# Mixing two token tiles side by side with the sines, and loading the first q and k in four halves

## The chip, the cores and the metric

The kernel runs on one core of one Trainium2 chip. The metric is the device time of one execution in microseconds (us); smaller is better. Seven runs of the kernel before gave a median of 173.86 us, from 173.14 to 174.23.

## The reference

Banded attention (a window of 96 tokens and 8 global tokens) with a linear distance bias, followed by a layer that mixes tokens through cosines and sines. Softmax is written here in one line:

```python
def _attn_ref(q, k, v, n_global, n_local):      # q, k, v: [4, 8, 768, 64] f32
    scores = scale * np.matmul(q, k.transpose(0, 1, 3, 2))
    rel = pos[:, None] - pos[None, :]
    is_global = pos[None, :] < int(n_global)                 # 8
    is_local = (rel >= 0) & (rel < int(n_local))             # 96
    keep = is_global | is_local
    dist = np.where(is_global & ~is_local, float(n_local), np.abs(rel))
    scores = scores - slopes[:, None, None] * dist
    a = softmax of scores where keep
    return np.matmul(a, v)

x = attention output, heads side by side                     # [4, 768, 512]
theta = x @ w_theta
zr, zi = x * np.cos(theta), x * np.sin(theta)
y = einsum('ts,bsd->btd', w_tok_r, zr) + einsum('ts,bsd->btd', w_tok_i, zi)
u = x + y
return u + np.maximum(u @ w_ch, 0.0)
```

## The kernel before

There are four batches, eight heads in four pairs, and six token tiles of 128. Matrix work is in bf16. The kernel is a software pipeline: batch 0's attention runs first alone; then each batch's token mixing is interleaved with the next batch's attention.

*The opening (lines 97 to 145 and 519 to 550).* Two hardware queues load q and k of batch 0's heads 0 and 1 in f32: k on SyncE's queue (SP), q on ScalarE's (ACT), line 99. Everything else comes through GpSimd's queue (POOL), cast to bf16 on the way: the other heads' q and k, v in two halves (line 88), then the weights (lines 154 to 161), then q, k and v of batches 1 and 2 (lines 73 and 88). VectorE (DVE) builds distance tables. `cast0` makes bf16 of the first pair, one head on DVE and one on ACT; `turn0` transposes on TensorE (PE); `out0` copies the transposed pair out of PSUM; `kglob` makes copies of k with the global tokens in front (kG). `score_bias` puts the bias into PSUM by a matmul, `score_mms` adds the scores, `score_exp` takes the exp on ACT. A pair of heads has three chunks of scores.

*Attention of batch 0 (lines 551 to 585)* is a hand-written order. `vglob` makes vG, the copy of v with global tokens; it waits for v. `values` multiplies by v, divides by the sum (rec, L364) and writes x_sb (L366). `xtrans` transposes x_sb.

*Handover (lines 586 to 599).* `trans_w(0)` transposes the token weights of tile 0 (12 transposes on PE into two PSUM tiles, one copy each into w_tokT, L168). `theta(b, c, j)` makes theta for the token tile pair c (L398); for j = 1 or 3 it goes on with the sines on ACT (cs, L404) and the products with x on DVE (zri, L408). The hand-written order ends here; in the rest of the kernel a scheduler puts the instructions of each engine in order by the priorities of the program's text. `weave` sets this text order for batch 0's mixing (`main`) and batch 1's attention (`side`): it interleaves the two lists by weights, and starts `side` after a share s0 of `main`.

*Mixing.* `mix(b, tt, g)` adds four matmuls (L419) of tile tt to one PSUM tile; after three of them DVE adds x (u, L424). `utrans` transposes u, `chan` multiplies by w_ch (L447), adds u and stores (o_sb, L452; the store is issued on SP, L454). For batch 0, `trans_w(tt + 1)` follows the second part of tile tt's mix; for tiles 1 and 2 both copies are on DVE, for tiles 3 to 5 one is on ACT.

*Attention of batches 1 to 3.* `prep` turns q and k of a pair: copies on DVE (qkn, L231), transposes on PE, copies out on DVE (qT, L250) and ACT (kT, L252), then kG (L220, L222). After the exp, DVE multiplies by a table of the bias (e, L315 and L318). For these batches x_sb is transposed by a DMA issued on SP (L370). `theta(1, 0, 0)` needs the first three of the four transposed head pairs, `theta(1, 0, 1)` the fourth.

*PSUM* holds eight banks: the pool `big` has two buffers of two banks (scores, values of batches 1 to 3, theta of tile pairs 0 and 1), the pool `small` four buffers of one bank (everything else). A buffer is reused when its last reader is done.

Of the kernel before, what the change touches and what calls it, by code (L numbers as in the profile page):

```python
# [16 lines left out]
def kernel(  # L17
# [77 lines left out]
        mybir.EngineType.Pool, mybir.EngineType.SP}))  # L95

    qk32 = moe.tile([T, 2, 2, NT, D], FP, name="qk32", tag="zri", bufs=1)
    for i_, eng in ((1, nc.sync), (0, nc.scalar)):
        eng.dma_start(out=qk32[:, i_].rearrange("p h t d -> p h (t d)"),
                      in_=(q, k)[i_][0, 0:2].rearrange("h (p t) d -> p h (t d)", p=T))  # L100
    near = const.tile([T, 2 * T], FP)
    nc.gpsimd.iota(near, pattern=[[1, 2 * T]], base=0, channel_multiplier=-1,
                   allow_small_or_imprecise_dtypes=True)
# [56 lines left out]
                w_nat[wi, tt], w_nat[wi, tt + 1] = w2[:, 0], w2[:, 1]  # L160
        nc.gpsimd.dma_start(out=w_ch_bf, in_=moe_w_ch.rearrange("(c p) n -> p c n", p=T))

    def trans_w(tt, copy=nc.vector.tensor_copy):
        for wi in range(2):
            ps = ps_small([T, NT, T], BF)
            for st in range(NT):
                nc.tensor.transpose(ps[:, st, :], w_nat[wi, tt][:, st * T:(st + 1) * T], ident)
            (copy if wi else nc.vector.tensor_copy)(out=w_tokT[wi][:, :, tt * T:(tt + 1) * T], in_=ps)  # L168


# [212 lines left out]
    def theta(b, c, j):  # L383
        last0 = [(j_, NC - 1) for j_ in range(2)]
        part = {0: [(0, dc) for dc in range(NC - 1)],
                1: [(1, dc) for dc in range(NC - 1)] + last0,
                2: [(j_, dc) for j_ in range(2) for dc in range(NC - 1)],
                3: last0}[j]
        if c == 0 and j in (0, 2):
            zri[b] = moe.tile([T, 2, NT, DM], BF, name="zri", tag="zri", bufs=1)  # L390
        xT, xb = xT_sb[b], x_sb[b]
        last = c == NT // 2 - 1
        if j in (0, 2):
            pss["th", c] = [ps_small([T, DM], FP) for _ in range(2)] if last else ps_big()
        pb = pss["th", c]
        st = lambda j_: slice((2 * c + j_) * T, (2 * c + j_ + 1) * T)
        for j_, dc in part:
            nc.tensor.matmul(pb[j_] if last else pb[:, j_, :], lhsT=xT[:, dc, st(j_)],  # L398
                             rhs=w_theta_bf[:, dc, :], start=(dc == 0), stop=(dc == NC - 1))
        if j in (1, 3):  # L400
            cs = moe.tile([T, 2, 2, DM], BF, name="cs")
            for i_, bias in ((0, {"bias": halfpi}), (1, {})):
                for o, p_ in [(cs[:, i_, j_], pb[j_]) for j_ in range(2)] if last else [(cs[:, i_], pb)]:
                    nc.scalar.activation(o, p_, AF.Sin, **bias)  # L404
            n = 2 if b else 1
            for i_ in range(2):
                for j_ in range(0, 2, n):
                    nc.vector.tensor_mul(  # L408
                        zri[b][:, i_, 2 * c + j_:2 * c + j_ + n, :].rearrange("p j (g d) -> p j g d", g=NP),
                        xb[:, :, 2 * c + j_:2 * c + j_ + n, :].rearrange("p g j d -> p j g d"),  # L410
                        cs[:, i_, j_:j_ + n].rearrange("p j (g d) -> p j g d", g=NP))

    def mix(b, tt, g):
        if g == 0:
            pss["mix"] = ps_small([T, DM], FP)
        ps = pss["mix"]
        for st in (2 * g, 2 * g + 1):
            for wi in range(2):
                anchor["pe"] = nc.tensor.matmul(  # L419
                    ps, lhsT=w_tokT[wi][:, st, tt * T:(tt + 1) * T], rhs=zri[b][:, wi, st, :],  # L420
                    start=(st == 0 and wi == 0), stop=(st == NT - 1 and wi == 1)).ins
        if g == NT // 2 - 1:
            u_sb[b, tt] = moe.tile([T, DM], BF, name="u", bufs=6)
            anchor["dve"] = nc.vector.tensor_add(  # L424
                u_sb[b, tt].rearrange("p (g d) -> p g d", g=NP), x_sb[b][:, :, tt, :],
                ps.rearrange("p (g d) -> p g d", g=NP)).ins
# [99 lines left out]
    distances()  # L526
    diagonals(0)
    score_bias(0, 0)
    score_bias(0, 1)
    cast0(1, dve, 0)  # L530
    bias_table(0)
    cast0(1, act, 1)
    turn0(0, 1)
    cast0(0, dve, 0)
    cast0(0, act, 1)
    turn0(0, 0)
    diagonals(1)
    out0(0, 1, act, 0)
    out0(0, 1, dve, 1)
    out0(0, 0, act, 1)  # L540
    out0(0, 0, dve, 0)
    kglob(0, 0, 0, 1, act)
    score_mms(0, 0, 0)
    kglob(0, 0, 1, NT - 2, act)
    score_exp(0, 0, 0)
    turn0(1, 1)
    turn0(1, 0)
    score_mms(0, 0, 1)
# [42 lines left out]
    theta(0, 1, 2)  # L591
    xtrans(0, p, dve, 4, 6)
    theta(0, 0, 3)
    theta(0, 1, 3)
    theta(0, 2, 2)
    theta(0, 2, 3)
    for h in range(1, H):
        bias_table(h)
    manual.close()
# [4 lines left out]
    for b in range(B):  # L604
        nxt = b + 1 if b + 1 < B else None
        lag = 3
        th = [lambda c=c, j=j: theta(b, c, j) for c in range(NT // 2) for j in range(2)]
        pre = [lambda p=p: prep(1, p) for p in range(NP)] if b == 0 else []
        ahead = [[lambda p=p: prep(2, p) for p in range(NP // 2)], [lambda p=p: prep_dma(3, p) for p in range(1)],
                 [], []][b]  # L610
        order = rest[:1] + th[:4] + rest[1:2] + th[4:] + rest[2:] if b else []
        if b == 2:
            order[:0] = [lambda p=p: prep_dma(3, p) for p in range(1, NP)]
        if b == 1:
            order.insert(0, lambda: load_behind(3, xT_sb[1][0:1, NC - 1, 0:1]))
        for f in order:
            f()
        main = []
        for tt in range(NT):
            for g in range(NT // 2):  # L620
                if (b, tt) != (B - 1, NT - 1):
                    main.append((2048, lambda tt=tt, g=g: mix(b, tt, g)))
                if b == 0 and g == 1 and tt + 1 < NT:
                    main.append((1536, lambda tt=tt: trans_w(tt + 1, nc.scalar.copy if tt > 1 else nc.vector.tensor_copy)))
                if tt >= lag and g == 0 and (b, tt) != (B - 1, NT - 1):
                    main.append((2048, lambda tt=tt: chan(b, tt - lag)))
                if b == 0 and tt and g == 1:
                    main.append((512, lambda tt=tt: utrans(b, tt - 1)))
            if b and (b, tt) != (B - 1, NT - 1):
                main.append((0, lambda tt=tt: utrans(b, tt)))  # L630
        side = [(1536, f) for f in pre]
        if b == 0:
            side[:0] = [(0, lambda: load_all_v(2))]
            side.append((0, lambda: (alloc_qk(3), load_qk_tokens(3, 0, H // 2))))
        side += attention_steps(nxt, ahead) if nxt else []
        weave(main, side, 0.3 if b == 0 else 0.0, 0.9)
        rest = [lambda tt=tt, b=b: chan(b, tt) for tt in range(NT - lag, NT)]
        if b == 0:
            rest.insert(1, lambda b=b: utrans(b, NT - 1))
# [44 lines left out]
```

The softmax here doesn't subtract the row's maximum and nothing guards it: scores larger than these inputs give would overflow.

## Time and profile before

| what | value |
|---|---|
| median of 7 runs | 173.86 us |
| the profiled execution, its own time | 173.69 us |
| its span in the profile | 171.6 us |
| PE busy | 159.8 us (93%), 1534 matmuls |
| DVE busy | 124.8 us (73%) |
| ACT busy | 101.3 us (59%) |
| POOL busy | 39.8 us (23%) |
| granted PE clock | full |
| moved by DMA | 25.93 MB, mean 151 GB/s |
| chain that ended last | PE 61%, DVE 16%, DMA 9%, ACT 7%, POOL 4% |
| costliest line | L419 (mix), 288 matmuls of 380 ns |

A line of a timeline gives the start, the duration (of the group, if several are merged), the engine, the line of the kernel, the operation, what is written from what, and in brackets the idle time before it and what ended it. A matmul's duration is that of its whole passage; matmuls overlap, so the spacing of their starts says what one costs. In a line of stretches the engines' busy times stand in the order PE, PE weight loads, DVE, ACT, POOL, then the granted clock, the DMA share and GB/s. Times on the timeline count from the start of the span.

### The profile page before, as it was taken

Reading aid. Unit: us, or ns where it says so; the run is one execution under the profiler, and the core shown is the slowest. Engines: PE = TensorE matmul, PEld = TensorE weight load, DVE = VectorE, ACT = ScalarE, POOL = GpSimd, SP = SyncE. Lnnn points to the kernel's source line nnn. Section 1 sums busy time; section 2 is a strip of 40 time slices with the busy share of each in tenths; the row PEclk is TensorE's granted clock in tenths of the full one; section 3 lists DMA queues with packets and bytes.
Section 4 is the critical chain, followed back from the end, with each engine's and each line's share of the span. In section 5 each row is a group of like instructions: output and inputs, shape, how many; then the busy total and the mean of one; then the engine's idle time right before and its main releaser. Section 6 shows DMA issues by size and latency. Waiting matters only on the chain.

```text
span 171.6 us, 3733 instructions
## 1 busy us (share of the span) xinstructions
PE 159.8 (93%) x1534; PEld 84.1 (49%) x1534; DVE 124.8 (73%) x265; ACT 101.3 (59%) x130; POOL 39.8 (23%) x45
## 2 busy tenths in 40 slices
PE   7489889989999999999999999989999999999991
PEld 2255456445755565445555464434454644444440
DVE  6737877587999999787998788297786856624442
ACT  4698683999797596199954550979347309500010
POOL 8965437005094010299000000000000000000000
PEclk9999999999999999999999999999999999999999
DMA  4999999999999999999996577888245563323335
GB/s 154 193 170 178 208 210 208 205 204 177 155 204 181 177 138 195 157 123 165 167 128 115 138 172 168 123 152 245 33 78 139 94 157 89 122 49 103 96 92 183
DMA packets 75088, 25.93 MB, mean 151 GB/s; under 512 B 63168, under 2 KB 72128, under 8 KB 75072
## 3 DMA queue, kind: packets, MB, share of 16 engines
q0 software_dynamic: 45680, 12.45, 77.6%
q1 hardware_dynamic: 28976, 12.72, 33.4%
q10 hardware_dynamic: 416, 0.52, 0.9%
q8 instruction: 12, 0.20, 0.5%
q14 instruction: 4, 0.03, 0.1%
HBM read 25.69 MB, written 6.29 MB: 186 GB/s over the span
## 4 chain that ended last, share of the span: by engine, by line
PE 61%; DVE 16%; DMA 9%; ACT 7%; POOL 4%; issue 2%; DVEq 0%; SPq 0%; POOLq 0%
PE ps L419 31%; PE ps L447 10%; DMA vn<-in_v_dram 6%; PE pb L398 6%; PE pb L296 5%; PE pb L355 4%; ACT cs L404 4%; POOL qk L73 3%; DMA kT<-qk 2%; DVE qT L250 2%; PE ps L398 2%; DVE zri L408 2%; DVE o_sb L452 2%; ACT e L306 2%; PE ps L246 1%
## 5 line engine op out<-in xcount | busy, mean ns | idle before, releaser
L419 PE MATMUL ps<-zri,w_tokT 128*128 128x512 bf16 x288 | 71.1, 380 | 1.6 <-DVE zri L408 0.8
L306 ACT ACTIVATE e<-pb 128x1024 bf16<-128x1024 f32 (+1 forms) x48 | 43.7, 960 | 17.7 <-PE pb L296 17.1
L419 PEld LDWEIGHTS <-w_tokT 128*128 128x128 bf16 x288 | 26.0, 98 | 30.2 <-issue 2.4
L424 DVE TENSOR_TENSOR u<-x_sb,ps 128x512 bf16<-128x512 bf16 x24 | 16.4, 684 | 13.1 <-PE ps L419 13.1
L447 PE MATMUL ps<-w_ch_bf,uT 128*128 128x512 bf16 (+1 forms) x100 | 24.7, 371 | 0.0
L408 DVE TENSOR_TENSOR zri<-x_sb,cs 128x1024 bf16<-128x1024 bf16 (+1 forms) x30 | 16.7, 581 | 5.6 <-ACT cs L404 5.3
L404 ACT ACTIVATE cs<-pb,halfpi 128x1024 bf16<-128x1024 f32 x8 | 8.9, 1115 | 19.2 <-PE pb L398 19.2
L452 DVE SCALAR_TENSOR_TENSOR o_sb<-ps,u 128x512 f32<-128x512 f32 (+1 forms) x25 | 16.4, 663 | 3.6 <-PE ps L447 3.6
L296 PE MATMUL pb<-qT,kT 64*128 64x128 bf16 x224 | 15.1, 219 | 1.6 <-DVE qT L211 1.3
L315 DVE TENSOR_TENSOR e<-e,etab 128x1024 bf16<-128x1024 bf16 (+1 forms) x24 | 14.8, 619 | 2.3 <-ACT e L306 2.3
L438 ACT COPY uT<-ps 128x512 bf16<-128x512 bf16 x7 | 4.1, 587 | 20.6 <-PE ps L437 20.6
L296 PEld LDWEIGHTS <-kT 64*128 64x128 bf16 x224 | 8.7, 94 | 14.7 <-issue 11.8
L398 PE MATMUL pb<-w_theta_bf,xT 128*128 128x512 bf16 x64 | 15.0, 379 | 0.0
L355 PEld LDWEIGHTS <-e 128*128 128x128 bf16 x352 | 13.0, 97 | 3.8 <-issue 1.6
L398 PEld LDWEIGHTS <-xT 128*128 128x128 bf16 x96 | 9.0, 98 | 10.8 <-DMA xT<-x_sb 0.9
L447 PEld LDWEIGHTS <-uT 128*128 128x128 bf16 x100 | 9.2, 98 | 10.0 <-ACT uT L438 0.8
L88 POOL DMA_DIRECT2D vn<-in_v_dram x5 | 9.6, 1924 | 12.2 <-DVE vn L68 10.3
L296 PE MATMUL pb<-qT,kG 64*128 64x128 bf16 x128 | 11.6, 217 | 0.9 <-DVE rec L364 0.5
L366 DVE TENSOR_TENSOR x_sb<-pb,rec 128x768 bf16<-128x768 f32 x12 | 11.4, 954 | 0.4
L82 POOL DMA_DIRECT2D qk<-in_k_dram x8 | 8.8, 1095 | 6.0 <-DMA vn<-in_v_dram 6.0
L355 PE MATMUL pb<-vn,e 128*128 128x65 bf16 x168 | 9.9, 193 | 0.2 <-ACT e L306 0.2
L318 DVE TENSOR_TENSOR e<-e,etab 128x1024 bf16<-128x1024 bf16 x12 | 8.2, 687 | 2.4 <-ACT e L306 2.4
(73 smaller groups left out, 203.6 us busy)
## 6 DMA issues: line engine op xcount, KB each, us to landing
out_dram<-o_sb SPq DMA_DIRECT2D x23, 256.0 KB, 2.4
vn<-in_v_dram POOLq DMA_DIRECT2D x3, 768.0 KB, 22.5
qk<-in_q_dram POOLq DMA_DIRECT2D x2, 768.0 KB, 20.7
qk<-in_k_dram POOLq DMA_DIRECT2D x2, 768.0 KB, 23.2
w_nat<-in_moe_w_tok_r_dram POOLq DMA_DIRECT2D x3, 384.0 KB, 15.1
w_nat<-in_moe_w_tok_i_dram POOLq DMA_DIRECT2D x3, 384.0 KB, 14.3
vn<-in_v_dram POOLq DMA_DIRECT2D x2, 384.0 KB, 9.9
qk<-in_q_dram POOLq DMA_DIRECT2D x8, 96.0 KB, 9.5
```

Source lines behind the costliest of these rows:

```text
L296: nc.tensor.matmul(pb[:, hh, o:o + T], lhsT=lhsT, rhs=qT[R, (own, nxt)[part]], start=bool(b), stop=bool(b) or (jt == NT - 1 or (j == 1 and ...
L306: ins = nc.scalar.activation(e_c, pb[:, :, 0:n], AF.Exp, scale=scale).ins
L315: nc.vector.tensor_mul(e_c, e_c, tab[:, :, s0:s0 + n // T].rearrange("p a s n -> p a (s n)"))
L355: nc.tensor.matmul(o, lhsT=l_, rhs=r_, start=(i_ == 0), stop=(i_ == len(mms) - 1))
L366: nc.vector.tensor_mul(xv, po4[:, :, :, 0:D], rec.to_broadcast([T, n, nt, D]))
L398: nc.tensor.matmul(pb[j_] if last else pb[:, j_, :], lhsT=xT[:, dc, st(j_)], rhs=w_theta_bf[:, dc, :], start=(dc == 0), stop=(dc == NC - 1))
L404: nc.scalar.activation(o, p_, AF.Sin, **bias)
L408: nc.vector.tensor_mul(zri[b][:, i_, 2 * c + j_:2 * c + j_ + n, :].rearrange("p j (g d) -> p j g d", g=NP), xb[:, :, 2 * c + j_:2 * c + j_ ...
L419: anchor["pe"] = nc.tensor.matmul(ps, lhsT=w_tokT[wi][:, st, tt * T:(tt + 1) * T], rhs=zri[b][:, wi, st, :], start=(st == 0 and wi == 0), ...
L424: anchor["dve"] = nc.vector.tensor_add(u_sb[b, tt].rearrange("p (g d) -> p g d", g=NP), x_sb[b][:, :, tt, :], ps.rearrange("p (g d) -> p g ...
L447: nc.tensor.matmul(ps_c, lhsT=uT[:, dc, :], rhs=w_ch_bf[:, dc, i_ * n:(i_ + 1) * n], start=(dc == 0), stop=(dc == NC - 1))
L452: nc.vector.scalar_tensor_tensor(o_sb[:, cols], in0=ps_c, scalar=0.0, in1=u[:, cols], op0=ALU.max, op1=ALU.add)
```

## The change

The first q and k are loaded as four halves, q of both heads first, one head on each of the two queues; q is cast and turned ahead of k, and each is copied out of PSUM whole. In the handover `trans_w` gets a wide form: its two PSUM tiles lie in one buffer of `big`, and both copies are on DVE. The sines and products become a function of their own, `sines`. Token tiles 0 and 1 of batch 0 are mixed in turns in the hand-written order, with the weight transposes of tiles 1, 2 and 3 and the sines between them. The interleaved part begins with tile 2; for tiles 4 and 5 both copies are on DVE; `side` starts after 0.1 of `main` in place of 0.3.

```diff
--- before.py
+++ after.py
@@ -95,9 +95,10 @@
         mybir.EngineType.Pool, mybir.EngineType.SP}))
 
     qk32 = moe.tile([T, 2, 2, NT, D], FP, name="qk32", tag="zri", bufs=1)
-    for i_, eng in ((1, nc.sync), (0, nc.scalar)):
-        eng.dma_start(out=qk32[:, i_].rearrange("p h t d -> p h (t d)"),
-                      in_=(q, k)[i_][0, 0:2].rearrange("h (p t) d -> p h (t d)", p=T))
+    for i_ in range(2):
+        for h, eng in enumerate((nc.sync, nc.scalar)):
+            eng.dma_start(out=qk32[:, i_, h].rearrange("p t d -> p (t d)"),
+                          in_=(q, k)[i_][0, h].rearrange("(p t) d -> p (t d)", p=T))
     near = const.tile([T, 2 * T], FP)
     nc.gpsimd.iota(near, pattern=[[1, 2 * T]], base=0, channel_multiplier=-1,
                    allow_small_or_imprecise_dtypes=True)
@@ -160,11 +161,16 @@
                 w_nat[wi, tt], w_nat[wi, tt + 1] = w2[:, 0], w2[:, 1]
         nc.gpsimd.dma_start(out=w_ch_bf, in_=moe_w_ch.rearrange("(c p) n -> p c n", p=T))
 
-    def trans_w(tt, copy=nc.vector.tensor_copy):
-        for wi in range(2):
-            ps = ps_small([T, NT, T], BF)
+    def trans_w(tt, copy=nc.vector.tensor_copy, wide=False):
+        pb = big.tile([T, 2, 2 * 512], BF, name="pbw", tag="pb") if wide else None
+        tiles = [pb[:, wi, 0:S].rearrange("p (t n) -> p t n", t=NT) if wide else ps_small([T, NT, T], BF)
+                 for wi in range(2)]
+        for wi, ps in enumerate(tiles):
             for st in range(NT):
                 nc.tensor.transpose(ps[:, st, :], w_nat[wi, tt][:, st * T:(st + 1) * T], ident)
+            if not wide:
+                (copy if wi else nc.vector.tensor_copy)(out=w_tokT[wi][:, :, tt * T:(tt + 1) * T], in_=ps)
+        for wi, ps in enumerate(tiles if wide else ()):
             (copy if wi else nc.vector.tensor_copy)(out=w_tokT[wi][:, :, tt * T:(tt + 1) * T], in_=ps)
 
 
@@ -397,25 +403,29 @@
         for j_, dc in part:
             nc.tensor.matmul(pb[j_] if last else pb[:, j_, :], lhsT=xT[:, dc, st(j_)],
                              rhs=w_theta_bf[:, dc, :], start=(dc == 0), stop=(dc == NC - 1))
-        if j in (1, 3):
-            cs = moe.tile([T, 2, 2, DM], BF, name="cs")
-            for i_, bias in ((0, {"bias": halfpi}), (1, {})):
-                for o, p_ in [(cs[:, i_, j_], pb[j_]) for j_ in range(2)] if last else [(cs[:, i_], pb)]:
-                    nc.scalar.activation(o, p_, AF.Sin, **bias)
-            n = 2 if b else 1
-            for i_ in range(2):
-                for j_ in range(0, 2, n):
-                    nc.vector.tensor_mul(
-                        zri[b][:, i_, 2 * c + j_:2 * c + j_ + n, :].rearrange("p j (g d) -> p j g d", g=NP),
-                        xb[:, :, 2 * c + j_:2 * c + j_ + n, :].rearrange("p g j d -> p j g d"),
-                        cs[:, i_, j_:j_ + n].rearrange("p j (g d) -> p j g d", g=NP))
+        if j == 1:
+            sines(b, c)
+
+    def sines(b, c):
+        pb, xb, last = pss["th", c], x_sb[b], c == NT // 2 - 1
+        cs = moe.tile([T, 2, 2, DM], BF, name="cs")
+        for i_, bias in ((0, {"bias": halfpi}), (1, {})):
+            for o, p_ in [(cs[:, i_, j_], pb[j_]) for j_ in range(2)] if last else [(cs[:, i_], pb)]:
+                nc.scalar.activation(o, p_, AF.Sin, **bias)
+        n = 2 if b else 1
+        for i_ in range(2):
+            for j_ in range(0, 2, n):
+                nc.vector.tensor_mul(
+                    zri[b][:, i_, 2 * c + j_:2 * c + j_ + n, :].rearrange("p j (g d) -> p j g d", g=NP),
+                    xb[:, :, 2 * c + j_:2 * c + j_ + n, :].rearrange("p g j d -> p j g d"),
+                    cs[:, i_, j_:j_ + n].rearrange("p j (g d) -> p j g d", g=NP))
 
     def mix(b, tt, g):
         if g == 0:
-            pss["mix"] = ps_small([T, DM], FP)
-        ps = pss["mix"]
-        for st in (2 * g, 2 * g + 1):
-            for wi in range(2):
+            pss["mix", tt] = ps_small([T, DM], FP)
+        ps = pss["mix", tt]
+        for wi in range(2):
+            for st in (2 * g, 2 * g + 1):
                 anchor["pe"] = nc.tensor.matmul(
                     ps, lhsT=w_tokT[wi][:, st, tt * T:(tt + 1) * T], rhs=zri[b][:, wi, st, :],
                     start=(st == 0 and wi == 0), stop=(st == NT - 1 and wi == 1)).ins
@@ -526,23 +536,22 @@
     distances()
     diagonals(0)
     score_bias(0, 0)
-    score_bias(0, 1)
-    cast0(1, dve, 0)
     bias_table(0)
-    cast0(1, act, 1)
-    turn0(0, 1)
     cast0(0, dve, 0)
     cast0(0, act, 1)
     turn0(0, 0)
-    diagonals(1)
-    out0(0, 1, act, 0)
-    out0(0, 1, dve, 1)
-    out0(0, 0, act, 1)
-    out0(0, 0, dve, 0)
+    score_bias(0, 1)
+    cast0(1, dve, 0)
+    out0(0, 0, dve)
+    cast0(1, act, 1)
+    turn0(0, 1)
+    warm(2)
+    out0(0, 1, act)
     kglob(0, 0, 0, 1, act)
     score_mms(0, 0, 0)
-    kglob(0, 0, 1, NT - 2, act)
+    kglob(0, 0, 1)
     score_exp(0, 0, 0)
+    diagonals(1)
     turn0(1, 1)
     turn0(1, 0)
     score_mms(0, 0, 1)
@@ -591,9 +600,19 @@
     theta(0, 1, 2)
     xtrans(0, p, dve, 4, 6)
     theta(0, 0, 3)
+    sines(0, 0)
     theta(0, 1, 3)
     theta(0, 2, 2)
     theta(0, 2, 3)
+    trans_w(1, dve, True)
+    sines(0, 1)
+    for g in range(NT // 2):
+        for tt in range(2):
+            mix(0, tt, g)
+        if g < 2:
+            trans_w(2 + g, dve, True)
+        if g == 0:
+            sines(0, 2)
     for h in range(1, H):
         bias_table(h)
     manual.close()
@@ -616,16 +635,18 @@
         for f in order:
             f()
         main = []
-        for tt in range(NT):
+        for tt in range(0 if b else 2, NT):
             for g in range(NT // 2):
                 if (b, tt) != (B - 1, NT - 1):
                     main.append((2048, lambda tt=tt, g=g: mix(b, tt, g)))
-                if b == 0 and g == 1 and tt + 1 < NT:
-                    main.append((1536, lambda tt=tt: trans_w(tt + 1, nc.scalar.copy if tt > 1 else nc.vector.tensor_copy)))
+                if b == 0 and g == 1 and 4 <= tt + 2 < NT:
+                    main.append((1536, lambda tt=tt: trans_w(tt + 2)))
                 if tt >= lag and g == 0 and (b, tt) != (B - 1, NT - 1):
                     main.append((2048, lambda tt=tt: chan(b, tt - lag)))
-                if b == 0 and tt and g == 1:
+                if b == 0 and g == 1:
                     main.append((512, lambda tt=tt: utrans(b, tt - 1)))
+                if (b, tt, g) == (0, 2, 0):
+                    main.append((512, lambda: utrans(0, 0)))
             if b and (b, tt) != (B - 1, NT - 1):
                 main.append((0, lambda tt=tt: utrans(b, tt)))
         side = [(1536, f) for f in pre]
@@ -633,7 +654,7 @@
             side[:0] = [(0, lambda: load_all_v(2))]
             side.append((0, lambda: (alloc_qk(3), load_qk_tokens(3, 0, H // 2))))
         side += attention_steps(nxt, ahead) if nxt else []
-        weave(main, side, 0.3 if b == 0 else 0.0, 0.9)
+        weave(main, side, 0.1 if b == 0 else 0.0, 0.9)
         rest = [lambda tt=tt, b=b: chan(b, tt) for tt in range(NT - lag, NT)]
         if b == 0:
             rest.insert(1, lambda b=b: utrans(b, NT - 1))
```

## The prediction

> **What bounds the kernel now.** I read the slices of the page first, to see which engines are full where; then the busy time by stretch; then the chain of waits and the timeline around the places that the diff touches; last the landing time of single loads.
>
> ```profile
> PE   7489889989999999999999999989999999999991
> DVE  6737877587999999787998788297786856624442
> DMA  4999999999999999999996577888245563323335
> ```
>
> A slice is 171.6/40 = 4.29 us. The DMA engines are full up to slice 22, some 94 us; VectorE (DVE) is nearly full in slices 10 to 15, some 43 to 69 us; TensorE (PE) looks full from slice 10 on, but its busy time hides gaps. The stretches show who really is full:
>
> ```profile
> 36.00:42.00 6.00, 5.90 (x43) 2.91 (x41) 4.36 (x11) 5.97 (x10) 2.21 (x1) 1.00 1.60 192
> 42.00:48.00 6.00, 5.87 (x81) 4.58 (x79) 6.00 (x17) 4.43 (x8) 1.23 (x2) 1.00 2.84 162
> 48.00:54.00 6.00, 5.96 (x80) 3.14 (x78) 6.00 (x14) 5.51 (x7) 5.01 (x5) 1.00 1.38 201
> 54.00:60.00 6.00, 5.87 (x81) 3.27 (x78) 5.96 (x14) 3.81 (x5) 0.82 (x1) 1.00 2.38 172
> 60.00:66.00 6.00, 5.48 (x92) 3.96 (x87) 5.93 (x13) 5.91 (x9) 0.83 (x1) 1.00 2.03 144
> 66.00:72.00 6.00, 6.00 (x47) 3.17 (x45) 4.99 (x11) 1.61 (x3) 0.21 (x2) 1.00 1.40 205
> ```
>
> After the length come PE, PE weight loads, DVE, ScalarE (ACT), GpSimd (POOL). DVE works 23.89 of the 24 us from 42 to 66. PE is not full there: a 512-column matmul in a packed row costs 0.216 us (40 in 8.63 us in the chain), a transpose 0.056 (12 in 0.67), a score pair member 0.036 (14 in 0.50), a value matmul 0.0305 (22 in 0.67); the counts of the four stretches times these give some 21.1 us of 24. So batch 0's mix with batch 1's attention is a DVE stage.
>
> Two transfers stand as walls ahead of it.
>
> ```profile
> 18.12 0.43 DVE L336 COPY vG<-vn 128x1040 bf16<-128x1040 bf16 x1 [0.54 <-DMA vn<-in_v_dram]
> 22.21 0.87 POOL L73 DMA_DIRECT2D qk<-in_k_dram  x1 [0.99 <-DMA w_nat<-in_moe_w_tok_r_dram]
> 40.87 0.69 DVE L424 TENSOR_TENSOR u<-x_sb,ps 128x512 bf16<-128x512 bf16 x1 [0.40 <-PE ps L419]
> 41.48 1.16 DVE L231 COPY qkn<-qk 128x768 bf16<-128x768 bf16 x4
> ```
>
> ```profile
> qk<-in_k_dram POOLq DMA_DIRECT2D x1, 768.0 KB, 19.5
> ```
>
> First wall: DVE waits for v of heads 4 to 7 until 18.12 (and for heads 0 to 3 until 13.14, 1.18 us). Second wall: k of batch 1, issued at 22.21, lands 19.5 us later, at 41.71. Its reader is the second of the four qkn copies, at about 41.75: it came just in time, so the profile shows no wait for it.
>
> The end of the DVE stage hands over to PE:
>
> ```profile
> 67.95 0.96 DVE L366 TENSOR_TENSOR x_sb<-pb,rec 128x768 bf16<-128x768 f32 x1
> 71.09 3.62 PE L398 MATMUL pb<-w_theta_bf,xT 128*128 128x512 bf16 x16
> ```
>
> ```profile
> 71.26 3.45 PE pb L398 x16
> ```
>
> The last x_sb of batch 1 is done at 68.91; its DMA transpose lands 2.7 us later (71.65; the gate copy on POOL starts at 71.7). Theta's first six matmuls don't need it; the seventh, at 71.26 + 6 x 0.216 = 72.55, does. Slack 0.9 us. From there PE is packed to 104 us (counts give 31.4 of the 32 us after 72), so what the seventh matmul loses or gains, the end loses or gains.
>
> **What the Trainium skill says.** "DMA: Bandwidth & Descriptors", section "Issuing engines are not separate DMA queues": DMAs from several engines run on the same 16 DMA engines and interleave, so more queues only save issue time. The trace agrees: the two first loads, on two queues, land 4.2 and 4.6 us after one issue time. Four halves thus change the order of arrival, not the rate. "VectorE: DVE Perf Modes", section "Why PSUM operands drop a tier": a PSUM source costs a copy its fastest modes. The trace agrees: 768 bf16 columns take DVE 0.48 to 0.55 us from PSUM (L168) and 0.27 from SBUF (L231, start to start). "SBUF — State Buffer", section "SBUF: two separate sides": DVE and GpSimd share a port pair under an exclusive lock. The trace agrees: the small kG copy L222 takes 0.17 us, but 0.61 at 20.58 while POOL issues a load from 20.33 to 21.21. Such stalls are in the DVE time that I reuse below.
>
> **The change part by part.** *Opening.* q in two halves first, then k; q is cast and turned while k lands; each copied out whole (DVE 0.95 for q, ACT 0.79 for k) instead of in halves. Before, the first exp starts at 8.59. After: k lands at 5.0 to 5.3 as before, ACT casts k's half to 5.7 (0.46), PE turns it to 6.3 (12 in 0.43), ACT copies it out to 7.2 and its first kG to 7.7 (0.31 + 0.20), the last two score matmuls and the exp follow at 7.9: 0.7 us earlier. How a half load lands is not in the trace: at best q comes at half of the 4.6, at worst all four at 5.3; neither end matters, because DVE then waits longer for v at 13.1 (slack 1.18) and 18.1 (0.54). Gain taken: 0. If v came earlier, up to 0.7. The second load on ACT's queue costs one issue (0.48) ahead of the table load, which ends at 2.53; the first exp of the table waits for DVE to 3.66 anyway. SP has nothing else to issue until 53 us. The two extra warm-up matmuls lie under ACT's 0.79.
>
> *Handover.* The weight transposes of token tiles 1 to 3 go to the big PSUM pair and both copies to DVE; tiles 0 and 1 are mixed alternately. The big buffer is a new wait of PE, with the mix queued behind it: theta pair 0's buffer is free when ACT has read it (32.15), as PE ends theta at 32.24; pair 1's at 34.06, before PE comes to it at 34.7. Cost 0. The wide copy itself isn't in the trace; same size and source as L168, so 0.48 to 0.55, and I take 0.5. DVE from 31.27: four zri (to 32.94), two copies (33.9), four zri (35.4), two copies (36.4), four zri (37.9), two copies (38.9), u of tile 0 (39.6) and, after PE ends tile 1 at 39.65, u of tile 1 (40.5): 12 x 0.38 + 6 x 0.5 + 2 x 0.62 = 8.8 us of work with 0.4 of waits, against 10.2 us before. So the qkn copies come up at 40.5 instead of 41.48. PE comes to its first qkn transposes at 41.65 instead of 41.89 with 3 mix matmuls and 12 transposes more behind it: 0.24 + 0.65 + 0.7 = 1.6 us of lead. But the second qkn copy needs k of batch 1, at 41.71. DVE's lead of 1.0 us ends in a wait, with all later DVE work queued behind it, and PE waits for that work.
>
> *After the wall.* From the k copy (41.75) to the last x_sb (68.91) DVE takes 27.16 us now. By the instruction order of the changed kernel the same stretch holds one w_tokT copy more (tiles 4 and 5 put both copies on DVE; before, three tiles had one each: +0.48) and one o_sb more (chan of tile 2 comes ahead of the last x_sb: +0.60). ACT loses three copies of 0.70 to 0.80, which buys nothing, since DVE is the bound. Two waits appear, because a score chunk reuses the PSUM pair that x_sb frees: now the chunk behind the first x_sb is ready 1.65 us later (x_sb ends 55.93, exp ends 57.53), and DVE fills it with u, e and two qkn copies (55.92 to 57.79). In the new order it has e (0.60) and an o_sb that itself waits for matmuls put behind those scores: they end 1.05 us after x_sb, o_sb starts at 1.2 and ends at 1.8, a wait of 0.6. After the second x_sb DVE had o_sb, e, qkn, qT (2.2 us) to fill 1.6; now e and two qkn (1.0): another 0.6. Not all will show, as the 27.16 holds like delays; bounds 0 and 1.2, taken 0.9. Sum: 27.16 + 0.48 + 0.60 + 0.9 = 29.1; last x_sb at 70.85, transposed by 73.6, and 0.1 because an output store is issued on SP just ahead of it (one such issue takes 0.35 to 1.26). Theta's seventh matmul at 73.65 instead of 72.55: **+1.1 us**. PE's 1.6 us of lead is spent waiting there. Behind it the order of work is almost the same, so I carry 1.1 to the end. The profiled execution took 173.69 us (span 171.6 and 2.1 around it): 174.8; the median of the runs, 173.86, lies 0.17 above: 174.96. I say 174.9.
>
> **Rivals.** *The debt just cancels.* If the two new waits don't show, x_sb ends at 69.97, the transpose lands at 72.7, and the end moves by +0.2; if k also lands 0.5 us sooner, by -0.3. That gives 173.5 to 174.2. For it: ACT and PE are lighter, so exps may be ready early. Against it: the waits come from PSUM reuse, not from ACT's load.
>
> *PE's lead carries through: faster.* If k of batch 1 lands by about 40.8, or DVE's stretch is shorter than its sum, the limit is PE, which could be at theta's seventh matmul by 72.55 - 1.6 = 70.95, if x_sb were done by 68.2. It decides from x_sb at 69.3 down (transpose at 72.05, -0.5 us); at full price the end is 173.86 - 1.6 = 172.3, likely half of that. For it: the handover really gains 1 us on both engines. Against it: the load queue is full from the start, so k cannot come earlier because PE does.
>
> *The change is not what it says:* excluded, the order of instructions shows the two tiles' matmuls alternating.
>
> **How the numbers follow.** About 0.3% (0.52 us) is what a measurement can tell from no change. DVE debt, 174.4 to 176.0 (upper end: both waits in full, 0.3 more for a late k, 0.6 for the store on SP): 0.57. Cancel: 0.25. PE's lead: 0.18. So faster 0.18, same 0.25, slower 0.57. The range runs from 172.9, inside the PE case, to 176.0; about 0.08 lies below and 0.05 above.
>
> **What would show it.** Right: the first score exp near 7.9 but vG still released by v at 18.1; u of tile 1 done near 40.5; a new DVE wait for k until 41.7; DVE full to the last x_sb near 70.9, with waits for ACT's exps behind the first two x_sb; theta's seventh matmul waiting for xT. Wrong: k landing before 41; the last x_sb before 69.3; no gap of PE ahead of theta's seventh matmul; or a wait downstream of 73 us that differs between the two.

## The result, and the profile after

The changed kernel takes 176.32 us (median of 12 runs, 175.21 to 177.17), the kernel before 173.86. The ratio is 1.0134, with a 95% interval from 1.0113 to 1.0155: slower by 2.5 us, where +1.1 was forecast. The time lies just above the range (176.0). The profiled execution took 176.38 us (span 174.3) against 173.69 (span 171.6): 2.7 us more, so it shows the loss well.

The slices of the changed kernel, for the rows that were shown of before, with the granted clock of TensorE between them:

```profile
PE   7789889996899999989999999999999999999990
DVE  6647876797989999968897787398876866714442
...
PEclk9999999999789999999999999999999999999999
DMA  5999999999999999469999566779355383323334
```

Slices 10 and 11 are new: before, the clock row was all nines; here it falls to 7 and 8 tenths (a slice is 4.36 us: some 44 to 52 us, counted from slice 0). Slice 9 of the PE row, just ahead, shows 6 instead of 9. The stretches give the place (after the length: PE, PE weight loads, DVE, ACT, POOL, then the clock, the DMA share and GB/s):

```profile
42.00:48.00 6.00, 3.94 (x40) 3.11 (x38) 5.99 (x11) 2.21 (x5) 1.78 (x1) 0.81 2.92 158
48.00:54.00 6.00, 5.81 (x59) 3.29 (x58) 5.55 (x14) 3.78 (x6) 3.82 (x5) 0.91 1.34 203
54.00:60.00 6.00, 5.81 (x88) 3.40 (x85) 5.79 (x13) 4.98 (x7) 2.38 (x3) 1.00 3.28 150
60.00:66.00 6.00, 5.77 (x83) 3.41 (x78) 6.00 (x13) 3.57 (x5) 0.83 (x1) 1.00 2.03 165
66.00:72.00 6.00, 5.68 (x76) 3.79 (x77) 5.96 (x15) 4.89 (x8) 0.00 (x0) 1.00 0.70 115
```

From 42 to 48 PE does 40 matmuls in 3.94 us of busy time; before it did 81 in 5.87. DVE is as full as ever (5.99), but with 11 instructions instead of 17. A full DVE that does a third less has instructions that take longer. The timeline names them, and what POOL did beside them:

```profile
40.47 0.44 DVE L237 COPY qkn<-qk 128x768 bf16<-128x768 bf16 x1
40.63 0.10 DVE L68 MEMSET vn<- 128x48 bf16 x1
...
41.57 2.21 POOL L88 DMA_DIRECT2D vn<-in_v_dram  x1 [12.49 <-DVE qkn L237]
41.98 2.49 DVE L237 COPY qkn<-qk 128x768 bf16<-128x768 bf16 x3 [1.07 <-DMA qk<-in_k_dram]
...
44.00 0.51 PE L252 MATMUL ps<-ident,qkn 128*128 128x128 bf16 x6 [1.94 <-DVE qkn L237]
...
71.67 0.97 DVE L372 TENSOR_TENSOR x_sb<-pb,rec 128x768 bf16<-128x768 f32 x1
...
73.02 1.89 PE L404 MATMUL pb<-w_theta_bf,xT 128*128 128x512 bf16 x8
75.44 1.90 PE L404 MATMUL pb<-w_theta_bf,xT 128*128 128x512 bf16 x8 [0.53 <-DMA xT<-x_sb]
```

Three of the copies of L237 take 2.49 us, where four took 1.16 before. They run while POOL issues the load of v of batch 2, the third batch (41.57 to 43.78). The first of the three, read alone, takes 1.96 us (41.98 to 43.94), and PE's transposes of it start at 44.00 after 1.94 us of standing. In the kernel before the same issue ran earlier, beside the copies of w_tokT and a u:

```profile
38.30 0.10 DVE L68 MEMSET vn<- 128x48 bf16 x1
39.25 2.21 POOL L88 DMA_DIRECT2D vn<-in_v_dram  x1 [10.31 <-DVE vn L68]
```

The memset writes the columns of ones beside v in the buffer vn; the load may be issued once that is done, about 0.85 us later in both kernels (38.40 to 39.25; 40.73 to 41.57; the profile of after names the qkn copy that ended just before). The diff shows the call that holds this memset, `load_all_v(2)`, only as an unchanged line: it stands at the head of the list of side work of the first mix, and that list now starts behind u of tile 1 instead of behind u of tile 0. So the issue moved by 2.3 us, onto the second wall.

The end of the stage: the last x_sb ends at 72.64 instead of 68.91, and the theta matmul that waits for its transpose starts at 75.44 instead of 72.55, 2.9 us later. The chain that ended last passes through the same points (start, length, what):

```profile
22.44 19.52 DMA qk<-in_k_dram
41.98 2.49 DVE qkn L237 x3
...
72.66 2.73 DMA xT<-x_sb
```

The last term is a transfer as before (2.73 us); the loss of this stage lies ahead of it.

### The profile page after: what moved, and what is told of

Its sections match the earlier page's. It is cut to its first block, busy times and chain, and to the rows that moved or that the text cites. A ratio compares the mean times of both kernels' runs of the same rounds, so it can differ in the third digit from the quotient of the medians.

```text
span 174.3 us, 3738 instructions
## 1 busy us (share of the span) xinstructions
PE 161.8 (93%) x1536; PEld 85.0 (49%) x1536; DVE 128.1 (73%) x269; ACT 98.8 (57%) x124; POOL 38.3 (22%) x45
## 4 chain that ended last, share of the span: by engine, by line
PE 48%; DMA 22%; DVE 14%; ACT 7%; POOL 5%; issue 2%; DVEq 0%; SPq 0%; POOLq 0%; ACTq 0%
PE ps L429 27%; DMA qk<-in_k_dram 11%; PE ps L457 8%; DMA w_nat<-in_moe_w_tok_r_dram 7%; PE pb L302 4%; ACT cs L414 3%; PE pb L361 3%; POOL qk L73 3%; PE ps L252 2%; PE pb L404 2%; DVE e L321 2%; DVE qkn L237 2%; DMA kT<-qk 2%; POOL vn L88 2%; ACT e L312 2%
## 5 line engine op out<-in xcount | busy, mean ns | idle before, releaser
L302 PE MATMUL pb<-qT,kT 64*128 64x128 bf16 x224 | 15.7, 220 | 1.1 <-ACT e L312 0.6
L258 ACT COPY kT<-ps 128x768 bf16<-128x768 bf16 x8 | 6.4, 798 | 7.1 <-PE ps L252 7.0
L252 PE MATMUL ps<-ident,qkn 128*128 128x128 bf16 x96 | 8.1, 234 | 2.1 <-DVE qkn L237 2.1
```

Of the source, the lines that this page charges most:

```text
L302: nc.tensor.matmul(pb[:, hh, o:o + T], lhsT=lhsT, rhs=qT[R, (own, nxt)[part]], start=bool(b), stop=bool(b) or (jt == NT - 1 or (j == 1 and ...
```

## The experiments

Three theories were on the table. A: the loss beyond the forecast is the issue of v on POOL, which stretches the qkn copies, and PE's standing behind them. B: it is the forecast's DVE debt, only larger (more copies, or the two new waits for ACT's exps). C: it comes from the opening, whose loads shift everything behind them. Kernels of one series share the runs of the kernel before, whose median was 174.05 to 174.19 us.

### The issue of v put back ahead of the mix

```diff
 (changed kernel)
     theta(0, 2, 3)
+    load_all_v(2)
     trans_w(1, dve, True)
...
-            side[:0] = [(0, lambda: load_all_v(2))]
```

> The changed kernel, with only the reservation of batch 2's v (a memset on DVE, which releases the load's issue on POOL) moved up from behind u of tile 1 to the first products of the handover. Theory A (POOL's issue of that load, 41.57 to 43.78, holds the port that the qkn copies need; PE then stands 1.9 us and loses clock): the k copy takes 0.27 us again from about 42.0, PE's clock stays at 1.00 from 42 to 54, the last x_sb comes 1.5 to 2.5 us earlier (70.1 to 71.1), and the time is 174.0 to 174.9. Theory B (the order of work on DVE behind the k copy, with the extra w_tokT copy and o_sb, makes the loss): less than 0.6 us is won, 175.7 or more.

Measured: 175.31 us, ratio 1.0084 (1.0053 to 1.0115), against 1.0134 with the collision; the two intervals just touch. The timeline:

```profile
38.52 2.21 POOL L88 DMA_DIRECT2D vn<-in_v_dram  x1 [9.32 <-PE ps L429]
...
42.00 0.90 DVE L237 COPY qkn<-qk 128x768 bf16<-128x768 bf16 x3 [1.11 <-DMA qk<-in_k_dram]
...
69.27 0.97 DVE L372 TENSOR_TENSOR x_sb<-pb,rec 128x768 bf16<-128x768 f32 x1
70.81 1.26 SPq L376 DMA_TRANSPOSE xT<-x_sb  x1
...
73.71 1.90 PE L404 MATMUL pb<-w_theta_bf,xT 128*128 128x512 bf16 x7 [0.23 <-DMA xT<-x_sb]
```

The three copies take 0.90 us again, the clock stays at 1.00 in every stretch, and theta's waiting matmul comes at 73.71. That is 1.7 us earlier than in the changed kernel and 1.16 later than in the kernel before. The last x_sb ends at 70.24, inside the range of theory A; the time lies above A's range and below B's, so A holds for a part of the loss. The remaining 1.2 us of the median (175.31 less 174.12) agrees with the debt of 1.1 that was forecast, though not term by term (see below).

### The collision alone, in the kernel before

```diff
 (kernel before; the memset and load of v placed behind w_tokT's copies of tile 2)
+    def v2_late():
+        with tc.issue_after(anchor["w", 2]):
+            load_all_v(2)
...
-            side[:0] = [(0, lambda: load_all_v(2))]
+            side[:0] = [(0, v2_late)]
```

> The kernel before, with only that memset moved down behind the w_tokT copies of tile 2, so that POOL issues the load at about 41.4 in place of 39.25; all other engines keep their order. Theory A: the qkn copies stretch over POOL's issue (some 1.5 us), PE stands and its clock falls, and the time goes up by 1 to 2 us, to 174.9 to 175.9. Theory B: nothing to speak of, within 0.4 us of the kernel before.

Measured: 175.60 us, ratio 1.0091 (1.0057 to 1.0126). The order of the other engines' work is that of before. The timeline and the stretch:

```profile
41.40 2.88 DVE L231 COPY qkn<-qk 128x768 bf16<-128x768 bf16 x4
41.46 2.40 POOL L88 DMA_DIRECT2D vn<-in_v_dram  x1 [12.39 <-PE ps L419]
...
69.59 0.96 DVE L366 TENSOR_TENSOR x_sb<-pb,rec 128x768 bf16<-128x768 f32 x1
```

```profile
42.00:48.00 6.00, 4.69 (x57) 3.30 (x56) 6.00 (x14) 2.78 (x4) 1.86 (x1) 1.00 2.80 163
```

Four copies take 2.88 us instead of 1.16; the last x_sb ends at 70.55, 1.64 later than before, and the first sine after it starts at 74.66 instead of 73.02, 1.64 again. So this one issue in this place costs 1.6 us at that point of the records and 1.5 in the medians (175.60 less 174.12), with none of the rest of the change. A part of the 1.6 is made up later in the profiled execution: the mix that starts at 113.13 in the kernel before, after a wait of PE of 0.56 us for an o_sb, starts at 114.33 here without it, 1.2 later, and the whole execution took 0.8 us more (174.50, the fastest of its seven, against 173.69). The clock stays at 1.00 here: PE stood for 0.8 us, not 1.9. The first copy began 0.06 us ahead of the issue, and the issue took 2.40 us instead of 2.21: it looks as if the later of the two waits for the earlier, whichever it is.

### Opening and handover apart

The first kernel is the one before with the new opening, the second the changed kernel with the old one; everything else stays.

```diff
 (kernel before with the new opening)
-    for i_, eng in ((1, nc.sync), (0, nc.scalar)):
...
+    for i_ in range(2):
+        for h, eng in enumerate((nc.sync, nc.scalar)):
...
+    out0(0, 0, dve)
+    cast0(1, act, 1)
+    turn0(0, 1)
+    warm(2)
+    out0(0, 1, act)
```

> The kernel before with only the opening of the change (four half loads, q first, whole copies). Prediction's step: hidden behind v at 13.1 and 18.1 and behind k of batch 1; within 0.3 us of the kernel before. Theory C (the opening itself pushes the loads of POOL's queue back by some 0.25 us): 0.2 to 0.4 us slower, with v of heads 4 to 7 at 18.4 and k of batch 1 near 42.0.

> The changed kernel with the opening of the kernel before. Theories A and B both: as the changed kernel, 176.0 to 176.4. Theory C: 0.2 to 0.4 us better than the changed kernel.

Measured: the opening alone 175.07 us, ratio 1.0034 (1.0008 to 1.0060); the handover alone 175.81 us, 1.0116 (1.0083 to 1.0148). The handover carries most of the loss; its timeline has the same collision, and k lands no earlier although the opening is the old one:

```profile
41.67 2.21 POOL L88 DMA_DIRECT2D vn<-in_v_dram  x1 [12.48 <-DVE qkn L236]
42.08 2.48 DVE L236 COPY qkn<-qk 128x768 bf16<-128x768 bf16 x3 [1.08 <-DMA qk<-in_k_dram]
```

C is no more than a small part. But it isn't nothing: the opening, counted at 0, costs about 0.3% (0.6 us by the ratio, where theory C said 0.2 to 0.4), which its interval only just separates from zero.

### PE kept busy through the collision

```diff
 (changed kernel, between the transposes of q and k of batch 1's first heads)
+            if (b, p, i_) == (1, 0, 1):
+                warm(8)
```

> The changed kernel, with eight matmuls of zeros on PE between the transposes of q and k of batch 1's first pair, so that PE is not idle while DVE waits; the scheduler also moves a few neighbours. The collision of POOL and DVE stays. If the fall of PE's clock to 0.81 is a cost of its own, the clock stays at 1.00 from 42 to 54 and the time falls by 0.5 to 1 us against the changed kernel, to 1.007 to 1.010 of the kernel before. If the clock only follows from the wait and DVE's lateness sets the end, 1.011 to 1.015 as the changed kernel.

Eight matmuls on zeros, whose result nobody reads, fill PE's wait. Measured: 175.76 us, ratio 1.0088 (1.0057 to 1.0119), some 0.5% better than the changed kernel. The line of the filling, and the stretch:

```profile
41.82 1.89 PE L180 MATMUL ps<-zero 128*128 128x512 bf16 x8
```

```profile
42.00:48.00 6.00, 4.85 (x47) 3.00 (x47) 5.59 (x12) 2.35 (x5) 1.71 (x1) 1.00 2.79 162
```

The clock is 1.00 again, with the k copy as slow as before (PE gets it at 43.93). The last x_sb ends at 71.62 instead of 72.64. So in these two profiled executions about 1 of the 2.4 us that the collision adds to the DVE stretch (below) goes with PE's standing and the clock behind it. This isn't clean: the eight matmuls moved a few neighbours in the order as well. Nor do the times settle the clock's share. The ratio lies in the range expected of a clock with a cost of its own, but its interval still touches that of the changed kernel (1.0113 to 1.0155), and it equals that of the kernel with the issue moved away (1.0084) within the noise, though its last x_sb ends 1.4 us later than there. And the mean clock of the twelve runs of the changed kernel lies between 0.986 and 0.999, where the fall in the profiled one, 3.4 us at half rate, is worth 1% of the span (mean 0.990): at most three of the twelve had it in full, and the two with a mean of 0.999 took 175.66 and 176.36 us. Most of the loss is there without the fall.

### The debt, and the wall of k

```diff
 (on top of the early issue of v: w_tokT copies of tiles 4 and 5 shared with ACT)
-                    main.append((1536, lambda tt=tt: trans_w(tt + 2)))
+                    main.append((1536, lambda tt=tt: trans_w(tt + 2, nc.scalar.copy)))
```

> The kernel with batch 2's v reserved early (e1), and for token tiles 4 and 5 the second of the two w_tokT copies on ACT again. By the instruction order DVE has 0.96 us less to do ahead of the last x_sb of batch 1. If DVE's stretch behind the k copy sets the end (theory B for what is left of the loss), the last x_sb comes near 69.3 in place of 70.24, and the time falls by 0.6 to 1.0 us against e1, to 0.2 to 0.5 us above the kernel before. If DVE is not what counts, it stays at e1's time.

```diff
 (on top of the early issue of v: the load of w_ch put behind q and k of batch 1)
-        nc.gpsimd.dma_start(out=w_ch_bf, in_=moe_w_ch.rearrange("(c p) n -> p c n", p=T))
...
     load_all_qk(1)
+    nc.gpsimd.dma_start(out=w_ch_bf, in_=moe_w_ch.rearrange("(c p) n -> p c n", p=T))
```

> e1, with the load of w_ch put behind q and k of batch 1 in POOL's queue, so that k lands some 2.5 us earlier, near 39.3. If the second wall (k of batch 1) holds DVE back, DVE begins the k copy near 40.8 in place of 42.0, the last x_sb comes near 69.1, and the time falls by 0.8 to 1.2 us against e1, to about the kernel before. If DVE's lead were lost elsewhere too, less than 0.3 us.

> The kernel before, with only w_ch put behind q and k of batch 1. There DVE comes to the k copy at 41.75, just as k lands, so an earlier k buys nothing: within 0.3 us of the kernel before. A gain of 0.5 us or more would say that k held it back already.

Copies to ACT: 173.87 us, ratio 0.9978 (0.9959 to 0.9998), 1.4 us less than with the early issue of v alone, and more than the 0.6 to 1.0 expected. In the profile the last x_sb ends at 69.57 instead of 70.24, 0.67 earlier, and the transpose is no longer held up by an output store; theta now waits for the transposes of the last two pairs:

```profile
71.61 3.33 PE L404 MATMUL pb<-w_theta_bf,xT 128*128 128x512 bf16 x14 [1.02 <-DMA xT<-x_sb]
```

The two profiled executions differ by 0.97 us (174.99 and 174.02), near what two copies of 0.48 weigh; the medians differ by more, and I can't account for the other 0.4. Fewer copies on DVE is worth at least its sum: B is right for the part that A leaves.

k ahead of w_ch: 174.54 us, ratio 1.0033 (1.0012 to 1.0055) with the early issue of v, and 174.05, ratio 0.9995 (0.9969 to 1.0021), in the kernel before. In the first, DVE no longer waits for k; the next wait stands 0.5 us behind:

```profile
40.68 1.16 DVE L236 COPY qkn<-qk 128x768 bf16<-128x768 bf16 x4
...
42.36 0.96 DVE L255 COPY qT<-ps 128x768 bf16<-128x768 bf16 x1 [0.52 <-PE ps L251]
```

PE is in its mix until 41.82 and can't turn qkn sooner. So of DVE's 1.0 us of lead little is left either way: the last x_sb ends at 70.03 against 70.24, not near 69.1 as expected, and the medians differ by more (0.8 us). That profiled execution took 175.69, above its own median, so I don't read more from it. In the kernel before, k came just in time, and bringing it sooner changes nothing, as it must.

### All together, with the old and the new opening

Early issue of v, copies shared with ACT, k ahead of w_ch; once with the old opening, once with the new:

> All together: v of batch 2 reserved early, w_ch behind k, the ACT copies for tiles 4 and 5, and the opening of the kernel before. If the handover's lead is real and only the collision, the wall and DVE's debt hid it, the sum is 2.0 us below e1: the last x_sb near 68.2, theta's matmuls on the last head pair near 71.7, and a time 0.6 to 1.2 us below the kernel before. If something else holds the pipeline from 42 to 72, it is within 0.3 us of the kernel before or slower.

> The kernel with all three mends (v of batch 2 reserved early, w_ch behind k, ACT copies) and the opening of the change in place of the old one. If the opening is hidden, as the prediction has it, the same as with the old opening: 0.993 to 0.997 of the kernel before. If the opening costs what it seemed to cost alone (0.34%), 0.996 to 1.000.

Measured: 173.22 us with the old opening, ratio 0.9948 (0.9929 to 0.9967); 174.04 with the new one, 0.9994 (0.9978 to 1.0011). The first beats both kernels of this case. k early alone gained nothing in the kernel before, so it should be the handover that gains here, 0.95 us in the medians (174.17 less 173.22), once what it pushed into the way is moved out of it. The time is in the expected range; the path is not. The last x_sb ends at 69.43, not near 68.2, and theta waits for the transposes of x_sb by DMA:

```profile
71.36 3.33 PE L402 MATMUL pb<-w_theta_bf,xT 128*128 128x512 bf16 x14 [0.90 <-DMA xT<-x_sb]
```

The first sine behind it starts at 73.21, 0.2 us later than in the profile of the kernel before (73.02); only by the first sine of batch 3's theta is it ahead, at 141.47 against 141.76. So the profile does not show a gain at the handover, and where the 0.95 us of the medians arises stays open. Old against new opening, the two intervals lie apart: here the opening costs some 0.5%, more clearly than alone.

### The opening taken apart

```diff
 (kernel before, only the four half loads)
-        eng.dma_start(out=qk32[:, i_].rearrange("p h t d -> p h (t d)"),
-                      in_=(q, k)[i_][0, 0:2].rearrange("h (p t) d -> p h (t d)", p=T))
+            eng.dma_start(out=qk32[:, i_, h].rearrange("p t d -> p (t d)"),
+                          in_=(q, k)[i_][0, h].rearrange("(p t) d -> p (t d)", p=T))
```

> The kernel before, with only the loads of the first q and k in four halves, q first; the order of casts, transposes and copies stays. The opening as a whole measured 0.34% (0.08 to 0.60) above the kernel before. If the loads are its cost (more descriptors on the hardware queues ahead of POOL's loads, so that v comes later), 1.002 to 1.006 of the kernel before. If the order of the copies is, 0.998 to 1.001.

> The kernel before, with only the new order of the opening (q cast and turned first, each copied out whole, two warm-up matmuls), and the two whole loads. If the loads are the opening's cost, 0.998 to 1.001 of the kernel before; if the order of the copies is, 1.002 to 1.006. If neither comes out of the noise, the opening's cost stays open.

The second kernel has the new order, the whole copies and the two warm-up matmuls, but two whole loads. Measured: the halves 175.65 us, ratio 1.0056 (1.0020 to 1.0093); the order 174.66, 1.0017 (0.9996 to 1.0038). The intervals overlap. In the profile of the halves PE waits for k of the second head pair, whose load stands on another queue, and its 24 transposes take 1.49 us instead of 0.86, at a clock that has fallen to half:

```profile
9.43 1.49 PE L201 MATMUL ps<-ident,qk 128*64 128x128 bf16 x24 [0.87 <-DMA qk<-in_k_dram]
```

The changed kernel shows 0.30 us of this wait, the opening alone none, and in the kernel before there is none. This execution is the slowest of its seven (176.31) and the only one of those with half loads whose clock is at 0.50 from 10 to 15 us (with the old opening the handover alone shows 0.81 and 0.85 from 5 to 15). So this wait is no explanation for the other kernels. Nor does a later v: the second copy of vG starts between 17.84 and 19.67 in the six kernels with whole loads and between 18.29 and 20.02 in the eight with half loads.

One difference does part all fourteen profiles. From the first sine of batch 3's theta to the end of the span the kernels with half loads take 30.14 to 30.21 us, those with whole loads 29.76 to 29.84. The last instructions of DVE begin 25.35 us behind that sine in the changed kernel and in the kernel before, so the 0.35 us lie behind the compute: from the issue of the last store to the end of the span it is 3.1 us before and 3.4 after. The halves alone have it (30.21), the new order alone has not (29.82). So the half loads cost some 0.35 us at the end of the program, a good part of the opening's price (alone 0.6 by the ratio). What the program does there with two loads more, no run shows, and the rest of the price stays open.

## Why the prediction was right or wrong, point by point

**Direction and place: right.** Most of the loss lies between the second wall and theta's waiting matmul, and PE's lead is spent waiting there. DVE sets it for the most part; from 45.39 to 51.59 the chain of the changed kernel runs on PE, for some 3.4 us of that at half clock.

**The opening: half right.** The first exp starts at 8.25 instead of 8.59, 0.34 us earlier and not 0.7 (ACT waits 0.85 us for PE's transposes of k, and the copy out ends at 7.36). That gain ends at v as I said: vG is copied at 18.38, after a wait for v of 0.68. But the price of 0 was wrong. v itself came 0.26 us later than before (18.12), and the first product with the sines starts at 31.49 instead of 31.27, though v differs by more than that between kernels with the same loads. What does not vary is 0.35 us at the end of the program, which the half loads cost. Alone the opening costs 0.3%, inside what I called no change, but not free.

**The handover: right.** I gave 40.5 for the end of u of tile 1; it was 40.50 (39.02 plus 1.48). qkn came up at 40.47, PE at its first transposes at 41.56 (I said 41.65). The wide copies took 1.02 for two, as assumed (0.5 each). PE is busy for all of the 12 us from 30 to 42, so it did not stand for the big buffer.

**The second wall: right.** k landed at 41.96 (22.44 plus 19.52), and DVE's lead ended in a wait of 1.07 us.

**The failed step: "Such stalls are in the DVE time that I reuse below."** I had seen that a copy can be held up by an issue on POOL, and took it that the 27.16 us of the stretch after the wall already held its share. They held none of this one: in the kernel before, the issue ran from 39.25 to 41.46 and ended just as the qkn copies began at 41.48. The change moved its release, the memset, 2.3 us later, so that it ran from 41.57 to 43.78, across the copy of k for which everything was waiting. I followed every instruction that the diff changes, but not the one that headed the side list whose start the diff moved. The page "SBUF — State Buffer" of the Trainium skill, section "SBUF: two separate sides", which I had cited, says that the loser of the lock "fully blocks"; this trace agrees: a copy of 0.27 us, begun 0.41 us behind the start of the issue, took 1.96 us and ended at 43.94, just behind the end of the issue (43.78).

Its size: from the copy of k to the end of the last x_sb the changed kernel takes 30.66 us (41.98 to 72.64), with the issue moved away 28.24 (42.00 to 70.24). The difference is 2.42: 1.59 in the copies themselves (2.49 less 0.90), and 0.83 in the work behind them, where DVE waits for a PE that had stood and then ran at half clock (DVE is idle for 0.71 us of the stretch, against 0.04 without the collision). At theta's waiting matmul 1.73 of the 2.42 remain (75.44 less 73.71) and in the spans 1.4 (174.3 less 172.9). In the times it is 0.9 by the ratios (0.5%) and 1.3 by the medians, each less that of the kernel before in its series; in the kernel before the collision costs 1.5 to 1.6. So its price is 0.9 to 1.7 us, and the 1.4 us that the forecast lacked (176.32 less 174.96) lies within that.

**The DVE debt: right, but one term was empty.** 27.16 + 0.48 + 0.60 is 28.24, to the hundredth what the kernel without the collision shows. The hundredth is luck: DVE's busy time in the stretch grew by 1.24 (26.96 to 28.20) where the two terms make 1.08, and its idle time fell by 0.16. The 0.9 us for two new waits did not appear: in the changed kernel e starts behind the first x_sb at 61.91, directly behind o_sb, and behind the second at 64.88, directly behind qkn. I had the exps ready 1.65 us behind the x_sb as before; in the longer stretch the fill was long enough. In its place stand 0.29 of later k (42.00 against the 41.71 from which I counted) and about 0.6 for the output store on SP, which I had priced at 0.1: without the collision the transpose is issued at 70.81, 0.57 behind its x_sb. So the +1.16 at theta's matmul agrees with my +1.1 by terms that are only partly mine, and the agreement is in part luck. Nor does all that theta's matmul loses reach the end: of its 1.6 us in the kernel before with the late memset 1.2 were left at 114 us.

**The rivals.** The debt just cancelling (0.25) assumed x_sb at 69.97; without the collision it ended at 70.24, nearer to this than to the 70.85 of the forecast, and yet the store made up for it. PE's lead carrying through (0.18) failed at k, which did not land by 40.8; the kernel that made k early shows that the next limit, PE's own mix up to 41.8, stood half a microsecond behind.

**A reading that was off.** The nines of the DMA row end with slice 20, counted from 0, so the DMA engines are full to some 90 us, not 94. Nothing rests on it.

## What to carry to other kernels

When a change moves a step, list what the moved step releases, not only what it computes: here a memset of 0.1 us released a load whose issue of 2.2 us held a copy on DVE until it was over. Lay such issues beside work that is not on the path, or beside operations that wait anyway; the same issue, put 3 us earlier, cost nothing that the trace shows. And where a lead ends at the landing of a load, price the copy behind that load first, since everything on two engines waits for it. Last, look at the end of the program too: two loads more cost 0.35 us there, whatever they gained at the start.

## What the runs showed of the hardware that I had not expected

In two profiles TensorE's clock halved after a short stand. This is the changed kernel in single microseconds (the clock is the third number from the end):

```profile
43.00:44.00 1.00, 0.00 (x1) 0.01 (x1) 1.00 (x2) 0.00 (x0) 0.78 (x1) 1.00 2.61 156
...
45.00:46.00 1.00, 0.88 (x11) 0.61 (x9) 1.00 (x3) 0.34 (x1) 0.00 (x0) 0.83 4.30 135
46.00:47.00 1.00, 1.00 (x12) 1.00 (x11) 0.99 (x4) 0.00 (x0) 0.00 (x0) 0.50 2.46 158
...
49.00:50.00 1.00, 1.00 (x15) 0.79 (x14) 1.00 (x5) 0.00 (x0) 0.00 (x0) 0.96 1.29 208
```

PE stood from 42.06 to 44.00. The clock fell to 0.50 only at about 45.7, when PE was at work again, and came back at about 49: some 3.4 us at half rate. The page "TensorE: Matmul & The Clock Gate" of the Trainium skill, section "What's actually happening", speaks of a free-running window of about 3.4 us and of half rate after an idle window. The length of the slow phase agrees; that a stand of 1.94 us, a little over half a window, was enough does not. With the same stand in the kernel that has the old opening (1.94 us) the clock fell in the same way; with 0.8 us, and with the stand filled by matmuls on zeros, it did not fall. It is no rule, though: the mean clocks of the other runs of the changed kernel leave no room for the whole fall in most of them.

The DMA transpose of the last x_sb landed 2.7 us after its issue in the kernel before and in the changed one; in the kernel with all edits and the old opening the last but one, issued at 66.58, was still what theta waited for at 71.36, as far as the trace tells the two apart.
